# One VectorE operation of two operands in place of a cast and a copy, in the finish of a unit's maxima

## The chip, the cores and the metric

The kernel runs on one core of a Trainium2 chip. The metric is the device time of one execution in microseconds (us); of several executions of a kernel the median counts. A core has a matrix engine (PE; PEld is its loading of weights, which overlaps), a vector engine (VectorE, DVE), an engine for activations (ScalarE, ACT), a general one (GpSimd, POOL) and one that issues transfers (SyncE, SP). Each works through its own queue in order; between queues there are semaphores.

## What is computed

One block mixes an attention and a channel MLP by a gate computed per token, for 2048 tokens of 576 features:

```python
x = A_x
g = _sigmoid((x * gate_w).sum(-1, keepdims=True))
a = _A_ref(x, A_wqkv, A_wo)                 # 32 heads of 18, softmax over 2048 keys, output projection
b = _B_ref(x, B_w1, B_b1, B_w2, B_b2)       # layer norm, 576 -> 4608, tanh GELU, 4608 -> 576
return g * a + (1 - g) * b
```

Everything is float32. The change is in the softmax of the attention:

```python
scores = jnp.einsum("bhqd,bhkd->bhqk", q, k) * scale
p = _softmax(scores, axis=-1)
o = jnp.einsum("bhqk,bhkd->bhqd", p, v)
```

## The kernel before

Matmul operands are stored in a rounded 32-bit form (`F32R`). Where more precision is wanted a number is held as two parts: its rounding, and what the rounding left out. The rounding is done by writing to an `F32R` tile.

The attention is cut into 32 *units*: a pair of heads times a half of the 1024 + 1024 query rows. For each unit there are two passes over the scores.

- *Pass 1* (`s1_round`) finds each query row's largest score. A round is two matmuls (L229, one for each head) into PSUM banks, and for each a reduction on DVE (L231) that leaves the maximum over 512 keys in the small tile `m`. A unit has 32 rounds. After the last, `s1_finish` joins them: it reduces the four pieces of each row to one negated maximum `nm` (L239; 128 partitions by 16: two heads by 8 blocks of 128 rows), rounds it into `nmh` (L240), copies the rounded part into one half of `nm2` (L241) and writes the rest, `nm - nmh`, into the other half (L242). Later in PE's queue a transpose (L246) turns `nm2` into rows, ACT copies them out (L248) and two transfers put them below the queries in the tile `qa`.
- *Pass 2* (`s2`) computes the scores again (L272), now with these rows among its operands so that the maximum is taken off by the matmul itself, then the exponential on ACT (L275), and the product with the values on PE (L290).

The MLP runs in the same stretch of the program. Its pieces, the matmuls of the first layer (L492) and of the second (L580), fill PE between the attention's. From a piece of the first layer DVE adds a bias (L512), ACT takes a square and a tanh (L543, L545), and POOL does the products and the rounding in float32 on tiles of 128 x 512 (all recorded under L182). From the second layer DVE adds the result to a sum in `x` (L597), which frees the PSUM bank that PE wants for the next.

The order of all this is written out by hand: the loop over units and key blocks at the end of the function calls `half_round`, `fill`, `pv` and `run_due`, which take the next round, the next piece of the MLP and whatever has come due. Pass 1 runs ahead of pass 2 by a unit and a few rounds. `s1_finish` is put off by one such slot after the last round (`defer(1, ...)`), and its transpose is called from `ROWS` after the next products with the values. So on DVE the four operations of the finish stand behind the last L231 of their unit and ahead of, in most units, two L597 and the L231 of the next unit's first rounds. DVE serves them in this order, whatever comes late.

`nm`, `nm2` and `nmh` come from the pool `asm`, with two buffers each; `nmh` takes 64 bytes a partition for each buffer.

Of the kernel before, what the change touches and what calls it, by code (L numbers as in the profile page):

```python
# [8 lines left out]
F32 = mybir.dt.float32  # L9
F32R = mybir.dt.float32r  # L10
AF = mybir.ActivationFunctionType
ALU = mybir.AluOpType
# [4 lines left out]
P = 128  # L17
# [52 lines left out]
def gated_mix_kernel(ctx: ExitStack, tc: tile.TileContext, x, wqkv, wo, w1, b1, w2, b2, gate_w, out):  # L70
    nc = tc.nc
# [32 lines left out]
    asm = ctx.enter_context(tc.tile_pool(name="asm", bufs=2))  # L104
# [10 lines left out]
    def psum(pool):  # L115
        return pool.tile([P, TB], F32, name="ps")
# [3 lines left out]
    def score_bank():  # L120

        ring[0] += 1
        if not looped[0]:
            return psum(ps_s1 if ring[0] % (NS1 + 1) < NS1 else ps_o)
        return psum(ps_s1 if ring[0] % (NS1 + 2) < NS1 else ps_s2)
# [10 lines left out]
    def dma_r(queue, dst, src):  # L136

        queue.dma_start(dst.bitcast(F32), src)
# [6 lines left out]
    def defer(n, fn):  # L145
        later.append((slot[0] + n, fn))
# [86 lines left out]
    def s1_finish(u):  # L233

        m4 = M4.pop(u)
        nm = asm.tile([P, 2, 8], F32, name="nm")
        nm2 = asm.tile([P, 2, 2, 8], F32, name="nm2")
        nmh = asm.tile([P, 2, 8], F32R, name="nmh")
        nc.vector.tensor_reduce(nm, m4, axis=AX.X, op=ALU.max, negate=True)  # L239
        nc.vector.tensor_copy(nmh, nm)  # L240
        nc.vector.tensor_copy(nm2[:, :, 0, :], nmh.bitcast(F32))  # L241
        nc.vector.tensor_tensor(nm2[:, :, 1, :], nm, nmh.bitcast(F32), op=ALU.subtract)  # L242

        def rows():
            ps = score_bank() if looped[0] else psum(ps_a)
            nc.tensor.transpose(ps[:32, :P], nm2.rearrange("p a b c -> p (a b c)"), ident)  # L246
            mr = oe[:32, :P].bitcast(F32R)
            nc.scalar.activation(mr, ps[:32, :P], AF.Copy)  # L248
            qa = QA[u % 3]
            queue = nc.gpsimd if looped[0] and slot[0] - inflow[0] < BUSY else nc.sync  # L250
            for h in range(2):
                r = 64 * h + 54
                dma_r(queue, qa[r:r + 2, :].rearrange("b (t n) -> b t n", n=P), mr[16 * h:16 * h + 16, :].bitcast(F32))
        if looped[0]:
            ROWS.append(rows)
        else:
            defer(4, rows)
# [74 lines left out]
    def next_round():  # L332
        if rounds:
            u, r = rounds.pop()
            s1_round(u, r)
            if r == NR - 1:
                defer(1, lambda: s1_finish(u))
# [1009 lines left out]
```

## Time and profile before

| | |
|---|---|
| median of 3 runs | 2227.85 us (2227.79 to 2228.08) |
| the profiled execution's own time | 2229.34 us |
| its span, first to last instruction | 2227.6 us |
| PE busy | 2209.8 us (99%) |
| DVE busy | 1648.6 us (74%) |
| ACT busy | 1429.3 us (64%) |
| POOL busy | 1003.5 us (45%) |
| granted TensorE clock | 1.000 |

The span has three parts, by their engines' busy times: up to some 190 us the projections of the attention, from there to some 2120 us both passes with the MLP between, then the rest of the output projection. In the middle part PE is busy 1922.7 of 1930 us. Since matmuls are pipelined and their ends are modelled, a busy PE is not a PE that loses nothing; where it waits is better read from the chain of work that ended last, which goes back from the last instruction, at each step to what released it. In the lines of the profile `nm` stands for both `nm` and `nm2`, since buffer numbers are left out of the names.

### The profile page before, as it was taken

To read this page: it belongs to the slowest core of one execution; us is meant where nothing else is said; L and a number is where in the kernel's file an instruction comes from. 1 tells how busy PE (TensorE), PEld (TensorE's weight loads), DVE (VectorE), ACT (ScalarE), POOL (GpSimd) and SP (SyncE) were. 2 spreads that over 40 slices of the span, in tenths; PEclk is the share of its full clock that TensorE was granted. 3 is DMA by queue.
4 is the path that set the end of the run, shared out by engine and by line. 5 is a ranking of instruction groups with operands and counts; after the bars stand their busy time and mean duration, and the time that the engine had idled before them with its cause. 6 is when DMAs were issued, how large, how long until landed. Compare 5 with 4: busy or idle time off the path is not lost.

```text
span 2227.6 us, 51540 instructions
## 1 busy us (share of the span) xinstructions
PE 2209.8 (99%) x20528; PEld 1583.7 (71%) x20528; DVE 1648.6 (74%) x2888; ACT 1429.3 (64%) x2655; POOL 1003.5 (45%) x1001
## 2 busy tenths in 40 slices
PE   8999999999999999999999999999999999999999
PEld 7878666766667766777666776766776776777668
DVE  6675777777778778777777777777777777777734
ACT  4333777777776666666666666666665666666772
POOL 4321766666664444444444444444444444444710
PEclk9999999999999999999999999999999999999999
DMA  8867555444464533333354424232464323242264
GB/s 266 270 222 220 192 174 162 145 159 148 151 195 139 195 102 120 123 120 104 113 171 151 136 79 135 100 124 100 120 177 145 107 103 121 102 148 93 89 223 168
DMA packets 164119, 329.23 MB, mean 148 GB/s; under 512 B 56830, under 2 KB 84090, under 8 KB 153150
## 3 DMA queue, kind: packets, MB, share of 16 engines
q1 hardware_dynamic: 161782, 322.19, 44.6%
q8 instruction: 162, 2.65, 0.5%
q10 hardware_dynamic: 1968, 3.70, 0.5%
q14 instruction: 79, 0.65, 0.1%
q0 software_dynamic: 128, 0.03, 0.0%
HBM read 233.47 MB, written 96.17 MB: 148 GB/s over the span
## 4 chain that ended last, share of the span: by engine, by line
PE 92%; DVE 3%; DMA 1%; ACT 1%; issue 1%; POOL 1%; SPq 0%; ACTq 0%; DVEq 0%; POOLq 0%
PE ps L290 20%; PE ps L492 20%; PE ps L580 19%; PE ps L272 13%; PE ps L229 11%; PE ps L892 3%; PE ps L1227 2%; PE ps L913 2%; DVE m L231 1%; DMA x<-in_B_w_dram 1%; ACT zz L545 1%; POOL w L182 0%; PE ps L768 0%; DMA p<-in_A_wqkv_dram 0%; PE ps L895 0%
## 5 line engine op out<-in xcount | busy, mean ns | idle before, releaser
L231 DVE TENSOR_REDUCE m<-ps 128x1 f32<-128x512 f32 x2048 | 1312.4, 684 | 406.7 <-PE ps L229 387.8
L275 ACT ACTIVATE p<-ps 128x512 f32<-128x512 f32 x1048 | 566.9, 595 | 265.7 <-PE ps L272 259.5
L275 ACT ACTIVATE ring<-ps 128x512 f32<-128x512 f32 x1000 | 542.3, 596 | 292.1 <-PE ps L272 288.7
L492 PE MATMUL ps<-big,w 64*128 64x512 f32 x3708 | 569.4, 393 | 0.2 <-issue 0.2
L182 POOL TENSOR_SCALAR zz<-zz 128x512 f32<-128x512 f32 x288 | 178.3, 619 | 746.1 <-ACT zz L545 713.7
L580 PE MATMUL ps<-w,hh 64*128 64x288 f32 x4352 | 487.1, 294 | 1.0 <-DVE x L597 1.0
L272 PE MATMUL ps<-qa,ka 56*128 56x512 f32 x2048 | 460.4, 421 | 3.5 <-ACT p L275 1.7
L580 PEld LDWEIGHTS ps<-w,hh 64*128 64x128 f32 x4352 | 426.8, 186 | 28.9 <-DVE x L597 4.2
L229 PE MATMUL ps<-ka,qa 54*128 54x512 f32 x2048 | 435.1, 398 | 0.6
L492 PEld LDWEIGHTS ps<-big,w 64*128 64x128 f32 x3708 | 368.9, 187 | 68.2 <-issue 0.5
L182 POOL TENSOR_TENSOR zz<-zz,z 128x512 f32<-128x512 f32 x288 | 371.4, 1290 | 24.0
L272 PEld LDWEIGHTS ps<-qa,ka 56*128 56x128 f32 x2048 | 212.7, 184 | 209.2 <-DVE m L231 165.0
L580 PE MATMUL ps<-w,hl 64*128 64x288 f32 x2176 | 351.1, 292 | 0.8 <-POOL hl L182 0.8
L290 PE MATMUL ps<-p,vt 128*32 128x512 f32 x1968 | 239.2, 598 | 0.0
L229 PEld LDWEIGHTS ps<-ka,qa 54*128 54x128 f32 x2048 | 220.0, 185 | 25.1 <-DVE m L231 4.9
L580 PEld LDWEIGHTS ps<-w,hl 64*128 64x128 f32 x2176 | 234.7, 185 | 1.2 <-POOL hl L182 1.1
L290 PE MATMUL ps<-ring,vt 128*32 128x512 f32 x1872 | 227.6, 598 | 0.0
L182 POOL TENSOR_TENSOR hl<-zz,hh 128x512 fp32r<-128x512 f32 x136 | 176.7, 1299 | 11.3
L182 POOL TENSOR_TENSOR w<-x,w 128x576 fp32r<-128x576 f32 (+1 forms) x54 | 98.7, 1842 | 168.3 <-ACT w L396 147.9
L290 PEld LDWEIGHTS ps<-p,vt 128*32 128x32 f32 x1968 | 52.6, 109 | 111.9 <-issue 102.6
L290 PEld LDWEIGHTS ps<-ring,vt 128*32 128x32 f32 x1872 | 50.0, 109 | 106.3 <-issue 106.3
L597 DVE SCALAR_TENSOR_TENSOR x<-ps,x 128x288 f32<-128x288 f32 x256 | 104.1, 448 | 8.6 <-PE ps L580 8.6
(124 smaller groups left out, 1562.3 us busy)
## 6 DMA issues: line engine op xcount, KB each, us to landing
w<-w_scr SPq DMA_DIRECT2D x54, 1152.0 KB
w<-w_scr SPq DMA_DIRECT2D x108, 576.0 KB
x<-in_B_w_dram SPq DMA_DIRECT2D x72, 288.0 KB
w_scr<-w SPq DMA_DIRECT2D x18, 1152.0 KB
w_scr<-w SPq DMA_DIRECT2D x36, 576.0 KB
qa<-qk_scr SPq DMA_DIRECT2D x192, 72.0 KB
ka<-qk_scr SPq DMA_DIRECT2D x84, 144.0 KB
qk_scr<-hh SPq DMA_DIRECT2D x36, 256.0 KB
```

The lines of the kernel that those rows point to most:

```text
L182: fn(*args, **kw)
L229: nc.tensor.matmul(ps, qa[r0:r0 + 54, t * P:(t + 1) * P], ka[r0:r0 + 54, kb * TB:(kb + 1) * TB], start=True, stop=True)
L231: nc.vector.tensor_reduce(M4[u][:, h, t, kb:kb + 1], ps, axis=AX.X, op=ALU.max)
L272: nc.tensor.matmul(ps[h], ka[r0:r0 + 56, kc * P:(kc + 1) * P], qa[r0:r0 + 56, qb * TB:(qb + 1) * TB], start=True, stop=True)
L275: nc.scalar.activation(p_of(n)[:, qb, h], ps[h], AF.Exp, scale=SCALE)
L290: nc.tensor.matmul(OB[u][r:r + 32, :], v[:, k, 19 * h:19 * h + 32], p_of(c)[:, qb, h, :], start=(k == 0), stop=(k == NT - 1))
L492: nc.tensor.matmul(ps[h], wt[w_][r, c, :], y[r, c, :], start=(k == 0), stop=(k == 26))
L580: mm = nc.tensor.matmul(ps[nn][:, :ND], h_[r, tok], w_[p_][r, cs[nn]], start=(k == 0), stop=(k == 6 * G - 1))
L597: nc.vector.scalar_tensor_tensor(dst, ps[nn][:, :ND], 0.5, b2b[:, cs[nn]] if g == 0 else dst, op0=ALU.mult, op1=ALU.add)
L892: nc.tensor.matmul(ps, w_[:, c, ms], big[:, s_, :], start=(k == 0), stop=False)
L913: nc.tensor.matmul(ps[:, :ND], big[:, s_, tok], w_[:, c, cs], start=(k == 0), stop=False)
L1227: nc.tensor.matmul(ps[:, :ND], OT[b][2][:, s_, tok], w_part(w_, c)[:, cs], start=(k == 0), stop=(k == 13))
```

## The change

The rounded part of `nm` is no longer made in a tile of its own and copied. One operation takes the larger of `nm` and `nm`, which is `nm`, and writes it, in the rounded form, straight to its half of `nm2`. The subtraction reads the rounded part from there. The tile `nmh` is gone.

```diff
         nm = asm.tile([P, 2, 8], F32, name="nm")
         nm2 = asm.tile([P, 2, 2, 8], F32, name="nm2")
-        nmh = asm.tile([P, 2, 8], F32R, name="nmh")
         nc.vector.tensor_reduce(nm, m4, axis=AX.X, op=ALU.max, negate=True)
-        nc.vector.tensor_copy(nmh, nm)
-        nc.vector.tensor_copy(nm2[:, :, 0, :], nmh.bitcast(F32))
-        nc.vector.tensor_tensor(nm2[:, :, 1, :], nm, nmh.bitcast(F32), op=ALU.subtract)
+        nc.vector.tensor_tensor(nm2[:, :, 0, :].bitcast(F32R), nm, nm, op=ALU.max)
+        nc.vector.tensor_tensor(nm2[:, :, 1, :], nm, nm2[:, :, 0, :], op=ALU.subtract)
```

On DVE this is how the finish stands in its queue in the unit whose operations lie at 641 us in the profile, before. `nm_8788` is `nm2`, the `m` and `nm` with other numbers or none are the unit's maxima; in brackets is the engine whose semaphore an instruction waits for.

```order
L231 TENSOR_REDUCE m_7854<-ps 128x1 [waits PE_49] x8
L239 TENSOR_REDUCE nm<-m_7854 128x16 [waits DVE_49]
L240 CAST nmh<-nm 128x16 [waits DVE_49]
L241 COPY nm_8788<-nmh 128x2x8 [waits DVE_49]
L242 TENSOR_TENSOR nm_8788<-nm,nmh 128x2x8
L597 SCALAR_TENSOR_TENSOR x<-ps,x 128x288 [waits PE_49] x2
L231 TENSOR_REDUCE m_8815<-ps 128x1 [waits PE_49] x8
```

And in the changed kernel, where `nm_8774` is `nm2` and the lines below the change have numbers lower by two:

```order
L231 TENSOR_REDUCE m_7840<-ps 128x1 [waits PE_49] x8
L238 TENSOR_REDUCE nm<-m_7840 128x16 [waits DVE_49]
L239 TENSOR_TENSOR nm_8774<-nm 128x2x8 [waits DVE_49]
L240 TENSOR_TENSOR nm_8774<-nm,nm_8774 128x2x8 [waits DVE_49]
L595 SCALAR_TENSOR_TENSOR x<-ps,x 128x288 [waits PE_49] x2
L231 TENSOR_REDUCE m_8799<-ps 128x1 [waits PE_49] x8
```

One instruction fewer stands in the queue, and the subtraction, which waited for nothing, now waits on DVE's own semaphore. Nothing else is moved: on every engine all other instructions stand in the same order and wait for the same ones. Since `nmh` is gone, the tiles allocated behind its pool (`big`, the weights `w`, `z`, `zz`, `res` and a few more) lie 128 bytes lower in each partition.

## The prediction

> **What bounds the kernel now.** I read the page's busy times first, then the chain of work that ended last as a whole, then the tile `nm` (what the change touches), then the waits of PE, and last the chain and the timelines around single units. The page:
>
> ```profile
> PE 2209.8 (99%) x20528; PEld 1583.7 (71%) x20528; DVE 1648.6 (74%) x2888; ACT 1429.3 (64%) x2655; POOL 1003.5 (45%) x1001
> ...
> PE 92%; DVE 3%; DMA 1%; ACT 1%; issue 1%; POOL 1%; SPq 0%; ACTq 0%; DVEq 0%; POOLq 0%
> ```
>
> PE is the bound; DVE carries 3% of the chain, some 67 us. A shorter DVE operation is worth something only where it stands in that 3%. The four operations of a unit's finish, from the view of the tile (count, then ns min/median/max), and PE's wait on the last of them (total us, times, longest):
>
> ```profile
> L239 DVE TENSOR_REDUCE nm<-m x32: 219/220/221, 198.1 to 2114.5; 128x16 f32<-128x64 f32 x32
> L240 DVE CAST nmh<-nm x32: 174/175/1098, 198.3 to 2114.8; 128x16 fp32r<-128x16 f32 x32
> L241 DVE COPY nm<-nmh x32: 174/175/1366, 198.6 to 2115.3; 128x16 f32<-128x16 f32 x32
> L242 DVE TENSOR_TENSOR nm<-nm,nmh x32: 160/169/589, 198.6 to 2115.8; 128x16 f32<-128x16 f32 x32
> ```
> ```profile
> PE ps L246 <- DVE nm L242: 1.4, 4, 0.3
> ```
>
> The medians are small, but the maxima are 3 to 8 times as long, on 16 elements. So in some units something holds these operations up, and in four units PE stood waiting for the last. There are two kinds of unit. An ordinary one (DVE's timeline: start us, us; then the chain in the same stretch):
>
> ```profile
> 1557.38 0.17 DVE L240 CAST nmh<-nm 128x16 fp32r<-128x16 f32 x1
> 1557.59 0.17 DVE L241 COPY nm<-nmh 128x16 f32<-128x16 f32 x1
> 1557.68 0.17 DVE L242 TENSOR_TENSOR nm<-nm,nmh 128x16 f32<-128x16 f32 x1
> 1557.76 0.82 DVE L597 SCALAR_TENSOR_TENSOR x<-ps,x 128x288 f32<-128x288 f32 x2
> ```
> ```profile
> 1557.05 1.85 PE ps L290 x16
> 1558.90 0.22 PE ps L246
> ```
>
> L241 waits for L240 (0.21 us from start to start), L242 follows L241 without a wait after 0.09, and L597 after another 0.08. The chain here is PE alone: L246, the transpose that reads the result, comes 1.0 us after L242 ended (1557.85), behind sixteen matmuls of L290. And a disturbed unit, DVE and then POOL from their timelines:
>
> ```profile
> 641.21 1.10 DVE L240 CAST nmh<-nm 128x16 fp32r<-128x16 f32 x1
> 642.34 0.17 DVE L241 COPY nm<-nmh 128x16 f32<-128x16 f32 x1
> 642.43 0.59 DVE L242 TENSOR_TENSOR nm<-nm,nmh 128x16 f32<-128x16 f32 x1
> 642.94 0.81 DVE L597 SCALAR_TENSOR_TENSOR x<-ps,x 128x288 f32<-128x288 f32 x2
> ```
> ```profile
> 641.00 1.28 POOL L182 TENSOR_TENSOR zz<-zz,z 128x512 f32<-128x512 f32 x1
> 642.37 0.63 POOL L182 TENSOR_SCALAR hh<-zz 128x512 fp32r<-128x512 f32 x1
> ```
>
> The CAST began 0.21 us after a POOL operation and ended at 642.31, 0.03 after that POOL operation (642.28). The COPY began 0.03 us ahead of the next POOL operation and ran in its usual 0.17. The TENSOR_TENSOR began 0.06 behind it and ended at 643.02, 0.02 after it (643.00). So DVE and POOL exclude each other here, and whichever starts first is served first; this holds for the CAST and for the operation of two SBUF operands alike. Chain and PE's timeline of the same unit:
>
> ```profile
> 641.21 1.11 DVE nmh L240
> ...
> 642.34 0.17 DVE nm L241
> 642.52 0.50 DVE nm L242
> 643.02 0.73 DVE x L597 x2
> 643.75 1.21 DVE m L231 x2
> ...
> 645.00 0.40 PE ps L229
> ```
> ```profile
> 640.81 1.92 PE L290 MATMUL ps<-ring,vt 128*32 128x512 f32 x16
> 643.07 0.29 PE L246 MATMUL ps<-ident,nm 128*32 128x128 f32 x1 [0.34 <-DVE nm L242]
> ```
>
> Here the finish is on the chain from end to end: its lateness passes through two L597 and two L231, which free PE's banks, into the L229 at 645.00. I looked at the chain behind each of the 32 finishes: in four units it reads like this, with L242 costing 0.50; in two more (266 and 579 us) L242 is short and the delay is in L241; in the other 26 no line of the finish is on it.
>
> ```profile
> 1070.32 0.50 DVE nm L242
> ...
> 1497.29 0.50 DVE nm L242
> ...
> 1870.77 0.50 DVE nm L242
> ...
> 267.15 0.55 DVE nm L241
> ...
> 579.93 0.07 DVE nm L241
> ...
> 580.31 0.16 DVE nm L242
> ```
>
> **The change part by part.** *Removed:* L240 and L241. *Added:* one TENSOR_TENSOR max on the same 128x16, standing where L240 stood and waiting for the same reduction. The trace has no max of this form; the nearest row is L242, two SBUF operands of the same size: 0.17. Its output is now fp32r; whether that costs anything, the rows of two SBUF operands over 512 elements tell (mean ns after the bar and busy time), once with fp32r written and once with f32:
>
> ```profile
> L1150 DVE TENSOR_TENSOR big<-x,big 128x512 fp32r<-128x512 f32 x16 | 10.9, 684 | 0.0
> ...
> L242 DVE TENSOR_TENSOR nm<-nm,nmh 128x16 f32<-128x16 f32 x32 | 8.3, 259 | 0.0
> ...
> L1140 DVE TENSOR_TENSOR x<-x,den 128x512 f32<-128x512 f32 x10 | 6.8, 684 | 2.1 <-DMA den<-ot_scr 2.1
> ```
>
> 684 and 684, so it costs nothing. (The row of L242 between them serves below.) I take 0.17 for the max where POOL is quiet and, where POOL is ahead, "until 0.02 to 0.03 after POOL's end", as for CAST and L242. The bounds of that price: 0.16 (L242's minimum) and 1.10 (the CAST of 641); it is nearest to L242.
>
> *The added wait:* the subtraction now reads what the max wrote, so it waits for the max, which it did not do behind the COPY. It takes over the COPY's place: 0.21 after the start of an undisturbed max, 0.03 to 0.05 after the end of a late one. Behind it in DVE's queue stand the L597 or L512 and L231 shown, which then start 0.08 after it rather than after the COPY's 0.09 plus 0.08.
>
> Per unit this gives:
> - Ordinary (21 of 32, once the seven and the four below are taken off): DVE is free 0.09 earlier. The cover is PE's own queue, 1.0 us of it ahead of L246. Counted as nothing. If that cover were gone it would be 21 x 0.09 = 1.9 us.
> - Disturbed like 641 (four): the subtraction starts at 642.34 to 642.36, just ahead of POOL's 642.37, is not held up, and L597 starts at 642.43 rather than 642.94: 0.51 earlier. PE can use all of it: L246 would be reached 1.85 us after 640.81, the start of L290's sixteen, so at about 642.66, and subtraction plus transpose are then early enough. What is late next is the same chain through L597 and L231, still 0.8 behind an ordinary unit because the max is held up as the CAST was, so the L229 still waits on DVE and moves by the full 0.51. 4 x 0.51 = 2.06.
> - Three more with the same L242 of 0.59 (1007, 1434, 1807; with the four they make up L242's mean of 259 ns against its median of 169, 32 x 0.09 = 2.9 us = 7 x 0.41) gain 0.51 on DVE, but PE has 24 matmuls of L290 ahead of L246 there and the chain has only PE rows:
>
> ```profile
> 1434.60 0.59 DVE L242 TENSOR_TENSOR nm<-nm,nmh 128x16 f32<-128x16 f32 x1
> ```
> ```profile
> 1434.19 2.71 PE ps L290 x24
> 1436.90 0.23 PE ps L246
> ```
>
>   Nothing.
> - Units whose COPY was held up (266, 518, 579, 2114): now the subtraction is held up in its place, by the same POOL operation, and ends with it. Saved is what followed the COPY, about 0.07. On the chain in 266 and 579: 2 x 0.07 = 0.15.
>
> Sum: 2.06 + 0.15 = 2.2 us, 0.10%. The profiled execution took 2229.34 us with a span of 2227.6; the median of the runs is 2227.85, 1.5 lower, and I set the gain against it unscaled: 2225.6.
>
> The Trainium skill ("SBUF — State Buffer", Who interferes with whom) says that casts and copies in their two-port mode, and operations of two SBUF inputs against a GpSimd operation that reads SBUF, take a shared pair of ports under an exclusive lock for the whole instruction. The trace agrees on the two ends of 0.02 and 0.03 us above, and by that rule the change doesn't leave the contended path: one contender less, two remain. By the rule's "whole instruction", POOL's operation would also wait for the subtraction, from 642.37 to 642.51, 0.14 us; in seven units 1.0 us, and the sum, were all of it to reach PE, 1.2 in place of 2.2. Against that the trace has POOL's TENSOR_SCALAR of 642.37 at 0.63 us, started while the COPY ran, and the one for which DVE's COPY waited in the unit at 266 at 0.61, so I price POOL's loss at 0.02:
>
> ```profile
> 267.06 0.61 POOL L182 TENSOR_SCALAR zz<-zz 128x512 f32<-128x512 f32 x1
> ```
>
> **The rivals.**
> 1. *The subtraction loses the race.* The margin is 0.03 us at best. If an operation of two operands asks for the port a little later in its run than a COPY, or its wait on the max takes 0.05, POOL goes first, the subtraction ends at 643.02 as before and the four units gain nothing. Left are the 0.15: 2227.7. For it: no row shows a TENSOR_TENSOR winning by so little. Against it: the COPY did, from the same place.
> 2. *More of DVE's saving reaches the end.* DVE saves 21 x 0.09 + 7 x 0.51 + 4 x 0.07 = 5.7 us in all. If PE's banks are freed late in ordinary units too, all of that would give 2222.2, and the point half-way from the forecast 2223.9. Against it: the chain of 26 units without a row of the finish.
> 3. *Slower: the moved addresses.* The tile `nmh` is gone, so every tile allocated behind that pool (`big`, the weights `w`, `z`, `zz`) lies 128 bytes lower in each partition. If PE's reads or the loads of those tiles minded, the place would be L492, 20% of the chain, some 436 us. It decides from 0.5% there (2.2 us); 1% makes 4.4 - 2.2: 2230.0. Against it: buffers of one tile lie at many addresses, and no group on the page splits by buffer.
> 4. *No change at all*, because ACT or POOL is late next in the four units: 2227.8. Against it: the chain after 645.00 is PE.
>
> **How the numbers follow.** I give the forecast 0.52, the lost race 0.17, more than the sum 0.15, the addresses 0.10, nothing 0.06. The range runs from 2223.3, which takes in most of the second rival, to 2228.6, which takes in the first and the fourth and a little of the third; the forecast's own range is 2225.0 to 2226.3. 0.2%, 4.5 us, is about what a measurement of this kernel can tell from no change. Faster by more needs nearly all of DVE's saving: 0.10. Slower by more needs over 1.5% on L492: 0.05. Within: 0.85.
>
> **What would show it.** In the changed kernel's profile: 32 TENSOR_TENSOR of max with a median near 0.17 and a longest near 1.1; the subtraction near 0.17 with no 0.59 left in the units at 641, 1069, 1496 and 1870 (with 0.59 there the race was lost); L246 about 0.4 earlier in them and PE's wait on the subtraction, 1.4 us in four, gone; the chain still with the max on it in these four. Wrong would be: POOL's operations longer than 0.63 beside the subtraction, max operations held up in units that are ordinary now, or a changed mean of L492 or L580.

## The result, and the profile after

The changed kernel takes 2225.53 us (median; 2224.1 to 2227.0), the kernel before 2228.13 us in the runs beside it. The ratio is 0.9986, with a 95% interval of 0.998 to 0.9992: faster, by 2.6 us in the medians (1.8 to 4.5 us by the interval), and within the 0.2% that the prediction set as the bound of "no change". The forecast was 2225.6.

The span of the profiled execution is 2224.1 us, 3.5 less than before. The page's busy times and its chain, as of before:

```profile
PE 2206.3 (99%) x20528; PEld 1576.1 (71%) x20528; DVE 1642.5 (74%) x2856; ACT 1428.9 (64%) x2655; POOL 1003.0 (45%) x1001
...
PE 91%; DVE 3%; DMA 2%; ACT 2%; issue 1%; POOL 1%; SPq 0%; DVEq 0%; ACTq 0%; POOLq 0%
```

PE and POOL have as many instructions as before, DVE 32 fewer and 6.1 us less busy time. The view of the tile `nm` (ns min/median/max; line numbers are lower by two, so L239 is the max and L240 the subtraction):

```profile
L238 DVE TENSOR_REDUCE nm<-m x32: 220/220/222, 197.8 to 2111.3; 128x16 f32<-128x64 f32 x32
L239 DVE TENSOR_TENSOR nm<-nm x32: 174/176/1106, 198.1 to 2111.6; 128x16 fp32r<-128x16 f32 x32
L240 DVE TENSOR_TENSOR nm<-nm,nm x32: 174/176/1371, 198.3 to 2112.1; 128x16 f32<-128x16 f32 x32
```

The max is as long as the cast was and is held up as long in the worst unit. In the view of PE's waits, the row in which L246 waited four times for the subtraction, 1.4 us in all, has no successor. Each held-up operation still ends just behind an operation of POOL that was running when it began: 21 of 96 casts, copies and subtractions before (0.019 to 0.035 us behind), 14 of 64 in the changed kernel (0.019 to 0.034 us). Those that began with POOL idle, or in the last 0.10 us of its operation, were not held up in either trace. The disturbed unit that the prediction followed, DVE and then POOL:

```profile
640.35 0.22 DVE L238 TENSOR_REDUCE nm<-m 128x16 f32<-128x64 f32 x1
640.60 1.09 DVE L239 TENSOR_TENSOR nm<-nm 128x16 fp32r<-128x16 f32 x1
641.73 0.18 DVE L240 TENSOR_TENSOR nm<-nm,nm 128x16 f32<-128x16 f32 x1
641.82 0.82 DVE L595 SCALAR_TENSOR_TENSOR x<-ps,x 128x288 f32<-128x288 f32 x2
```
```profile
640.38 1.28 POOL L182 TENSOR_TENSOR zz<-zz,z 128x512 f32<-128x512 f32 x1
641.75 0.64 POOL L182 TENSOR_SCALAR hh<-zz 128x512 fp32r<-128x512 f32 x1
```

The subtraction starts at 641.73, 0.02 us before POOL's next operation, and runs its 0.18. Before, it started 0.06 behind that operation and took 0.59. From the start of the max to the start of the first L595 it is now 1.22 us; from the cast to the first L597 it was 642.94 - 641.21 = 1.73. PE in the same stretch, and the chain:

```profile
640.19 1.92 PE L288 MATMUL ps<-ring,vt 128*32 128x512 f32 x16
642.05 0.28 PE L244 MATMUL ps<-ident,nm 128*32 128x128 f32 x1
```
```profile
640.60 1.10 DVE nm L239
...
641.73 0.18 DVE nm L240
641.90 0.73 DVE x L595 x2
642.63 1.21 DVE m L231 x2
...
643.88 0.40 PE ps L229
```

The transpose follows 1.86 us behind the start of the sixteen matmuls, as in an ordinary unit, with no wait. The chain still runs through the finish, since the max is held up; only the half microsecond of the subtraction has left it.

Where along the program the time went is read from the 32 transposes: how much earlier each begins than in the trace of before, both counted from the start of the span. Over the four units (from the transpose before each to the one behind it) this "lead" grows by 0.51, 0.49, 0.53 and 0.47 us, together 2.0. The lead is 0.35 already at the first transpose, grows by 0.38 between 394 and 459 us, and by some 0.5 over everything else up to the last transpose; behind that come another 0.25. The second profile of the changed kernel, below, shows which of these belong to the change.

### The profile page after: what moved, and what is told of

Same layout as the page of the kernel before. It is cut to its first block, busy times and chain, and to the rows that moved or that the text cites. A ratio compares the mean times of both kernels' runs of the same rounds, so it can differ in the third digit from the quotient of the medians.

```text
span 2224.1 us, 51508 instructions
## 1 busy us (share of the span) xinstructions
PE 2206.3 (99%) x20528; PEld 1576.1 (71%) x20528; DVE 1642.5 (74%) x2856; ACT 1428.9 (64%) x2655; POOL 1003.0 (45%) x1001
## 4 chain that ended last, share of the span: by engine, by line
PE 91%; DVE 3%; DMA 2%; ACT 2%; issue 1%; POOL 1%; SPq 0%; DVEq 0%; ACTq 0%; POOLq 0%
PE ps L288 20%; PE ps L578 20%; PE ps L490 20%; PE ps L270 13%; PE ps L229 11%; PE ps L890 3%; PE ps L1225 3%; PE ps L911 1%; DVE m L231 1%; DMA p<-in_A_wqkv_dram 1%; ACT zz L543 1%; DMA x<-in_B_w_dram 1%; POOL w L182 0%; PE ps L766 0%; ACT p L273 0%
## 5 line engine op out<-in xcount | busy, mean ns | idle before, releaser
L229 PE MATMUL ps<-ka,qa 54*128 54x512 f32 x2048 | 433.1, 398 | 0.6
L288 PE MATMUL ps<-p,vt 128*32 128x512 f32 x1968 | 239.2, 598 | 0.0
L229 PEld LDWEIGHTS ps<-ka,qa 54*128 54x128 f32 x2048 | 217.1, 184 | 25.3 <-DVE m L231 5.2
L578 PEld LDWEIGHTS ps<-w,hl 64*128 64x128 f32 x2176 | 230.1, 185 | 1.2 <-POOL hl L182 1.1
L288 PE MATMUL ps<-ring,vt 128*32 128x512 f32 x1872 | 227.6, 598 | 0.0
L288 PEld LDWEIGHTS ps<-p,vt 128*32 128x32 f32 x1968 | 52.5, 109 | 112.1 <-issue 102.7
L288 PEld LDWEIGHTS ps<-ring,vt 128*32 128x32 f32 x1872 | 49.9, 109 | 106.5 <-issue 106.5
L595 DVE SCALAR_TENSOR_TENSOR x<-ps,x 128x288 f32<-128x288 f32 x256 | 104.1, 449 | 8.7 <-PE ps L578 8.4
```

What stands on the lines that cost most here:

```text
L229: nc.tensor.matmul(ps, qa[r0:r0 + 54, t * P:(t + 1) * P], ka[r0:r0 + 54, kb * TB:(kb + 1) * TB], start=True, stop=True)
L288: nc.tensor.matmul(OB[u][r:r + 32, :], v[:, k, 19 * h:19 * h + 32], p_of(c)[:, qb, h, :], start=(k == 0), stop=(k == NT - 1))
L578: mm = nc.tensor.matmul(ps[nn][:, :ND], h_[r, tok], w_[p_][r, cs[nn]], start=(k == 0), stop=(k == 6 * G - 1))
L595: nc.vector.scalar_tensor_tensor(dst, ps[nn][:, :ND], 0.5, b2b[:, cs[nn]] if g == 0 else dst, op0=ALU.mult, op1=ALU.add)
```

## The experiments

The theory is that of the prediction: 16-element operations of DVE and POOL's operations exclude each other, the first to start is served first, and the change gains because the subtraction takes the copy's place just ahead of POOL's next operation, in four units. The rivals: DVE's small saving adds up over the ordinary units; the two operands of the max matter; the moved addresses matter. For each run the table at the end has the time and the lead over the four units.

**Only the four units.** The new form where `u` is 7, 14, 21 or 27, the old one elsewhere:

```diff
+        nmh = asm.tile([P, 2, 8], F32R, name="nmh")
+        if u in (7, 14, 21, 27):
+            nc.vector.tensor_tensor(nm2[:, :, 0, :].bitcast(F32R), nm, nm, op=ALU.max)
+            nc.vector.tensor_tensor(nm2[:, :, 1, :], nm, nm2[:, :, 0, :], op=ALU.subtract)
+        else:
+            nc.vector.tensor_copy(nmh, nm)
...
```

> The new form in the four units at 641, 1069, 1496 and 1870 us alone, the old one in the other 28; addresses as before. Theory (the gain is the subtraction that gets ahead of POOL in these four, 0.51 us each): 2.05 us faster than before, 2226.1 beside 2228.1, and in the profile the 0.59 us subtraction gone in these four units only. Rival (DVE's 0.09 us saved in each of the ordinary units adds up): 4 of 32 units, at most 0.4 us faster, 2227.7.

It took 2226.35 us beside 2228.45, ratio 0.9991 (0.9982 to 0.9999): 2.1 us from 4 units of 32. By its interval alone this could also be the rival's 0.4 us; the trace decides. The lead grows by 0.58, 0.49, 0.50 and 0.51 over these four units and not at all (-0.06) over the rest outside the stretch at 394 to 459 us. The view of `nm` has short subtractions in the four and the long ones still elsewhere:

```profile
L242 DVE TENSOR_TENSOR nm<-nm,nm x4: 174/176/176, 642.0 to 1868.8; 128x16 f32<-128x16 f32 x4
L246 DVE TENSOR_TENSOR nm<-nm,nmh x28: 159/168/589, 198.7 to 2113.5; 128x16 f32<-128x16 f32 x28
```

So the theory holds, and the sum of ordinary units is not the main part.

**All but the four units.** The complement, with `if u not in (7, 14, 21, 27)`:

> The complement: the old form in those four units, the new one in the other 28. Theory: 0.15 us (the units at 266 and 579) to 0.6 us faster than before, 2227.5 to 2228.0, and the four subtractions of 0.59 us still there. Rival (the saving adds up over ordinary units): about 2 us or more faster, 2226.

2227.64 us, ratio 0.9996 (0.9987 to 1.0005); the medians differ by 0.8 us, a little more than the 0.6 that the theory allowed at most, and the interval holds that, zero, and the rival's 2 us as well. Again the trace decides: the lead grows by only 0.11 over the four units and by 0.7 over the rest. The four subtractions are as before (view of `nm`; in this kernel L246 is the subtraction of the old form):

```profile
L246 DVE TENSOR_TENSOR nm<-nm,nmh x4: 585/588/589, 641.8 to 1869.6; 128x16 f32<-128x16 f32 x4
```

The two halves, 2.1 and 0.8, make 2.9, against 2.6 to 2.8 for the whole change; the intervals are too wide for this sum to prove more than that nothing large is missing.

**The copy put back, behind the max.** It reads what the max wrote; nobody reads what it writes. So the rounding is made by the max, straight into `nm2`, and only the place in time of the subtraction is that of before:

```diff
+        junk = asm.tile([P, 2, 8], F32, name="junk")
...
         nc.vector.tensor_tensor(nm2[:, :, 0, :].bitcast(F32R), nm, nm, op=ALU.max)
+        nc.vector.tensor_copy(junk, nm2[:, :, 0, :])
         nc.vector.tensor_tensor(nm2[:, :, 1, :], nm, nm2[:, :, 0, :], op=ALU.subtract)
```

> The changed kernel with a copy put back between the max and the subtraction: it reads what the max wrote and writes a tile that nobody reads; addresses as before. Theory: the copy takes the place ahead of POOL's next operation, the subtraction comes 0.09 us later and loses the race, 0.59 us in the four units again, and the time is that of before, 2228.1 (2227.8 to 2228.4). Rival (what helps is that the max, with two operands, stands where the cast stood, or that nothing waits on two roundings): as fast as the change, 2225.5.

2228.52 us, ratio 1.0002 (0.9994 to 1.0011): all of the gain is gone. DVE and POOL in the first of the four units:

```profile
641.39 0.17 DVE L241 COPY junk<-nm 128x16 f32<-128x16 f32 x1
641.48 0.59 DVE L242 TENSOR_TENSOR nm<-nm,nm 128x16 f32<-128x16 f32 x1
641.99 0.81 DVE L597 SCALAR_TENSOR_TENSOR x<-ps,x 128x288 f32<-128x288 f32 x2
```
```profile
641.41 0.63 POOL L182 TENSOR_SCALAR hh<-zz 128x512 fp32r<-128x512 f32 x1
```

The copy starts 0.02 us ahead of POOL and runs, the subtraction starts 0.07 behind and waits. Nine hundredths of a microsecond in the subtraction's start decide over 0.4 in its length.

**A cast in place of the max.**

```diff
-        nc.vector.tensor_tensor(nm2[:, :, 0, :].bitcast(F32R), nm, nm, op=ALU.max)
+        nc.vector.tensor_copy(nm2[:, :, 0, :].bitcast(F32R), nm)
```

> The changed kernel with a one-operand cast from nm straight into its half of nm2 in place of the max of two operands. Theory (one operation fewer is what counts, and cast and max are held up by POOL alike): as fast as the change, 2225.5 (2225.0 to 2226.2), the longest cast 1.1 us. Rival (the two operands matter): back towards before, 2227 or more, or, if a cast is held up less, 2224 or less.

2225.45 us, ratio 0.9987 (0.9978 to 0.9996), as the change. The cast's minimum, median and maximum are those of the max to 2 ns:

```profile
L239 DVE CAST nm<-nm x32: 174/175/1104, 197.5 to 2111.2; 128x16 fp32r<-128x16 f32 x32
```

So the operation of two operands is not what helps. What helps is that the rounding is written where it is wanted, so that the copy can go.

**The old addresses.** `nmh` is allocated again and not used:

```diff
         nm2 = asm.tile([P, 2, 2, 8], F32, name="nm2")
+        asm.tile([P, 2, 8], F32R, name="nmh")
```

> The changed kernel with the tile nmh allocated again and not used, so that every address is that of before. Theory: the addresses cost and bring nothing, 2225.5 (2225.0 to 2226.2). Rival (the tiles that moved by 128 bytes have a part in the gain, or hide a larger one): away from 2225.5 by 0.5 us or more, 2228.1 if they are all of it.

2225.75 us, ratio 0.9989 (0.998 to 0.9997), beside 2225.66 for the changed kernel on the same chip. The lead over the four units is that of the change too (2.10 us). No effect of the 128 bytes shows.

**No operation that POOL can hold up.** In the kernel before, 14 of the 32 reductions L239 began while an operation of POOL ran, and none was held up: the longest is 221 ns against a minimum of 219. The Trainium skill ("SBUF — State Buffer", Who interferes with whom) says that on trn2 a `tensor_reduce` never contends with GpSimd. The trace agrees. So the whole finish was written in reductions. Rounding happens where a result is written, so a reduction can write the rounded part itself; and a difference is the sum of a pair, if one of the two is stored with its sign turned:

```diff
-        nm = asm.tile([P, 2, 8], F32, name="nm")
+        nm = asm.tile([P, 2, 8, 2], F32, name="nm")
...
+        nc.vector.tensor_reduce(nm[:, :, :, 0], m4, axis=AX.X, op=ALU.max, negate=True)
+        nc.vector.tensor_reduce(nm[:, :, :, 1].bitcast(F32R), m4, axis=AX.X, op=ALU.max)
+        nc.vector.tensor_reduce(nm2[:, :, 0, :].bitcast(F32R), m4, axis=AX.X, op=ALU.max, negate=True)
+        nc.vector.tensor_reduce(nm2[:, :, 1, :], nm, axis=AX.X, op=ALU.add)
```

> The finish made of four reductions, each with one operand: the negated maxima, their negative in rounded form and the rounded part, all three from the pieces, and the subtraction as a sum over pairs. If POOL excludes DVE only where DVE reads two operands or copies (theory), none of these is held up: the longest is as the median, about 0.2 us, and the four units lose their remaining 0.8 us as well, the unit at 266 another 0.8: 2225.5 - 4 x 0.8 - 0.8 = 2221.5 (2221 to 2223). Rival (any DVE operation on that memory is held up beside POOL, or the wait isn't on POOL at all): operations of 0.5 to 1.1 us remain, and with four in place of three the time is 2225.5 or above.

2221.6 us beside 2228.44, ratio 0.9968 (0.9956 to 0.998). That beats both kernels: its slowest run, 2222.70, is below the fastest of the changed kernel on the same chip, 2224.69. The theory's 2221.5 was met. The tile's view, then DVE, POOL and the chain in the first of the four units:

```profile
L238 DVE TENSOR_REDUCE nm<-m x32: 220/220/222, 198.6 to 2107.3; 128x16 f32<-128x64 f32 x32
L239 DVE TENSOR_REDUCE nm<-m x32: 207/209/213, 198.7 to 2107.5; 128x16 fp32r<-128x64 f32 x32
L240 DVE TENSOR_REDUCE nm<-m x32: 208/209/212, 198.8 to 2107.6; 128x16 fp32r<-128x64 f32 x32
L241 DVE TENSOR_REDUCE nm<-nm x32: 174/177/181, 199.0 to 2107.7; 128x16 f32<-128x32 f32 x32
```
```profile
640.28 0.22 DVE L238 TENSOR_REDUCE nm<-m 128x16 f32<-128x64 f32 x1
640.41 0.21 DVE L239 TENSOR_REDUCE nm<-m 128x16 fp32r<-128x64 f32 x1
640.54 0.21 DVE L240 TENSOR_REDUCE nm<-m 128x16 fp32r<-128x64 f32 x1
640.66 0.18 DVE L241 TENSOR_REDUCE nm<-nm 128x16 f32<-128x32 f32 x1
640.76 0.81 DVE L596 SCALAR_TENSOR_TENSOR x<-ps,x 128x288 f32<-128x288 f32 x2
```
```profile
640.30 1.28 POOL L182 TENSOR_TENSOR zz<-zz,z 128x512 f32<-128x512 f32 x1
641.67 0.62 POOL L182 TENSOR_SCALAR hh<-zz 128x512 fp32r<-128x512 f32 x1
```
```profile
640.19 1.85 PE ps L289 x16
642.05 0.21 PE ps L245
642.26 0.42 PE ps L271
```

All four reductions run beside POOL's operation of 1.28 us, for which the cast and the max had to wait. Of the 128 in the trace 60 began beside a running POOL operation, and none takes over 222 ns. The first L596 starts 0.48 us after the first reduction, against 1.47 in the change, and the chain there is PE alone. The lead grows by 1.45, 1.48, 1.41 and 1.41 over the four units, and by 0.82 over the unit at 266, where the change had gained 0.05. Four operations in place of three cost less than one wait. A little of the gain is not POOL's: the second and third reduction need not wait for the one ahead (0.13 us from start to start), while the max starts 0.25 us behind the reduction that it reads.

**One contended operation left.** Only the rounded part is written by a second reduction; the subtraction keeps its two operands:

```diff
-        nc.vector.tensor_tensor(nm2[:, :, 0, :].bitcast(F32R), nm, nm, op=ALU.max)
+        nc.vector.tensor_reduce(nm2[:, :, 0, :].bitcast(F32R), m4, axis=AX.X, op=ALU.max, negate=True)
```

> The rounded part is written by a second reduction of the pieces, which waits for nothing new; the subtraction stays an operation of two operands and alone can be held up. Theory: in the four units the subtraction now begins beside POOL's first operation and ends with it, 0.02 us after, so the operations behind it start about 0.2 us earlier than in the change, in the unit at 266 about 0.6: 2225.5 - 0.8 - 0.6 = 2224.1 (2223.5 to 2224.8). Rival (it is the number of operations on DVE that counts, three as in the change): 2225.5.

2224.68 us, ratio 0.9983 (0.9974 to 0.9992), 1.0 us less than the change beside it and at the upper end of what was expected. In the unit shown before (DVE, POOL):

```profile
639.98 0.97 DVE L240 TENSOR_TENSOR nm<-nm,nm 128x16 f32<-128x16 f32 x1
640.88 0.81 DVE L595 SCALAR_TENSOR_TENSOR x<-ps,x 128x288 f32<-128x288 f32 x2
```
```profile
639.64 1.28 POOL L182 TENSOR_TENSOR zz<-zz,z 128x512 f32<-128x512 f32 x1
```

The subtraction is now the one that waits, and it ends at 640.95, 0.03 after POOL's 640.92. The lead grows by 0.74, 0.75, 0.66 and 0.67 us in the four units and by 0.65 in the unit at 266: 0.8 and 0.6 more than in the change, the sizes expected. That the median moved by only 1.0 of these 1.4 us is within its interval; it was not followed further.

**The changed kernel again.**

> The changed kernel again, beside the three above on the same chip: 2225.5, for the comparison. A second profile of it tells which of the differences between the two profiles so far belong to the change (the four steps of 0.5 us, by the theory) and which change from execution to execution (0.3 us before the first finish, 0.4 us between 392 and 456 us, 0.3 us at the end).

2225.66 us, ratio 0.9987 (0.9979 to 0.9996). The four steps are there again (0.50, 0.50, 0.47, 0.43). The lead at the first transpose is 1.52 us this time, against 0.35, with the same kernel; over the nine profiles it lies between 1.52 ahead and 0.47 behind. The step between 394 and 459 us was 0.38 and is now 0.18; with the old addresses the trace loses 0.58 there, and the kernel with the copy gains 0.48. These two vary from execution to execution, so nothing is read from them here; why they vary was not looked into.

All runs together, with the lead summed over the four units from the traces:

| kernel | median, us | ratio to before (95%) | lead over the four units, us |
|---|---|---|---|
| the change | 2225.53 | 0.9986 (0.998 to 0.9992) | 2.00 |
| the change again | 2225.66 | 0.9987 (0.9979 to 0.9996) | 1.90 |
| the four units alone | 2226.35 | 0.9991 (0.9982 to 0.9999) | 2.09 |
| all but the four | 2227.64 | 0.9996 (0.9987 to 1.0005) | 0.11 |
| the copy put back | 2228.52 | 1.0002 (0.9994 to 1.0011) | 0.17 |
| cast for max | 2225.45 | 0.9987 (0.9978 to 0.9996) | 2.00 |
| old addresses | 2225.75 | 0.9989 (0.998 to 0.9997) | 2.10 |
| reductions alone | 2221.60 | 0.9968 (0.9956 to 0.998) | 5.75 |
| one contended left | 2224.68 | 0.9983 (0.9974 to 0.9992) | 2.81 |

## Why the prediction was right

*The price of the max* was put at 0.17 us and up to 1.10; the median is 0.176 and the longest 1.106. The 1.28 us of POOL's operation hold it up as they held the cast.

*The race.* It was forecast that the subtraction would start 0.01 to 0.03 us ahead of POOL; it was 0.02 (641.73 against 641.75), in all four units and in the three others of that kind, where L240 takes 0.17 to 0.18. The rival in which the race is lost had 0.17 of the chances, and the copy put back shows what it would have cost: everything. The prediction rested on this margin more than on anything else. The traces show something that it didn't see: the margin is small but not a matter of chance. Both starts follow from the end of the same POOL operation: the max ends 0.03 us behind it and the subtraction starts 0.03 later, while POOL's own next operation starts 0.09 behind it. So the margin is 0.019 to 0.025 us in all 28 such units of four traces (the change twice, the cast, the old addresses).

*The full 0.51 reaches PE.* Measured 0.47 to 0.53 a unit, 2.0 in all against 2.06; in the second profile 0.43 to 0.50, 1.9 in all. The L229 behind it still waits on DVE, as the chain shows.

*The three units with 24 matmuls of L288 ahead of the transpose* gained as much on DVE and nothing at the transpose: from the transpose before to their own the lead changed by -0.06, 0.00 and 0.01 us.

*Ordinary units at nothing, 0.15 for 266 and 579.* This part of the sum may have been too small, and it is not settled. The kernel with the new form in all but the four units is 0.8 us faster in the medians, with an interval that holds zero; outside the four units and the stretch at 394 to 459 us its lead grows by 0.7 between the first and the last transpose. In the changed kernel the same measure gives 0.5 in the first profile and 0.2 in the second; in the kernel with the copy put back, whose subtractions start as before, it gives 0.2. The 0.07 for the unit at 266 can't be told from nothing: the lead there grows by 0.05, and by 0.06 with the copy put back. The chain of the unit at 579 no longer has the finish on it:

```profile
578.84 1.85 PE ps L288 x16
580.69 0.23 PE ps L244
...
581.11 1.13 ACT zz L543 x2
```

What that unit gained falls into the stretch counted to the unit at 641. That stretch's 0.51 is no more than the 0.58 of the kernel in which 579 kept the old form, so no gain shows there. Some tenths of a microsecond probably come from units that were priced at nothing; which of them was not tried. The second rival (more of DVE's saving reaches the end) is true to that extent at most: of DVE's 5.7 us some 2.0 to 2.5 arrived.

*POOL's loss* was put at 0.02 us from its rows: POOL's operation behind the subtraction took 0.64 us, against 0.62 for the same one in the kernel of reductions, where nothing stood in its way; its start is not put off either, 0.09 us behind POOL's operation before in both. (The 0.64 is a hair above the 0.63 that the prediction named as a sign of being wrong, with no effect on the time.) By the rule of the Trainium skill ("SBUF — State Buffer", Who interferes with whom) that the pair of ports is held for the whole instruction the loss would by estimate be 0.16, from POOL's start to the subtraction's end. The row decides: of the 0.18 us recorded for the subtraction, POOL's operation shows 0.02.

*The addresses*, the slower rival, show no effect: the mean matmul of the first layer, where the rival's loss would lie, is 392 ns after and 393 before, that of the second layer 294 in both. The chain behind the four units was not stopped by ACT or POOL.

*The number* was in part luck. The sum gave 2.2 us, taken from a median of 2227.85; measured were 2.6 us against 2228.13. The two differences, 0.4 and 0.3, nearly cancel, so that forecast and result lie 0.1 us apart, where the interval of the gain is 2.7 us wide. What the runs bear out is the mechanism and its main term, 2.0 of 2.06 us.

## What to carry to other kernels

A small operation whose longest instance is several times its median is probably held up by something outside it; look for what another engine did at that moment, and count only the instances that stand on the chain, which here were four of the seven held-up subtractions. Removing an operation then is worth what it moves the next one ahead of, so a margin of hundredths of a microsecond can carry the whole gain, and one more operation ahead of it can lose it. It is safer to use a form that was not held up at all: rounding in the reduction that makes the value, and a difference as a sum of pairs, gave 6.8 us where the change gave 2.6.

## What was not expected of the hardware

Reductions of 64 elements that wait for nothing start 0.13 us apart though each takes 0.21 to 0.22, and a reduction that writes the rounded form is shorter than one that writes float32 (209 against 220 ns in the medians of the kernel of reductions; the first of a row may pay for being the first, which was not separated). And the held-up operation pays almost nothing beyond the wait itself: it ends 0.02 to 0.04 us after POOL's in all nine traces that have one, though undisturbed it takes 0.17. The profile's page calls POOL's spans rough, but these differences repeat to some hundredths of a microsecond.
